# Sixteen stores of converted weight quarters moved out of block 0, and the slots of the preparing work set anew

## The chip, the cores and the metric

The kernel runs on one core of a Trainium2 chip. The metric is the device time of one execution in microseconds (us). The core's engines run their own instruction queues: TensorE (PE) multiplies, VectorE (DVE) and ScalarE (ACT) do elementwise work, GpSimd (POOL) helps with elementwise work between tiles on chip, and SyncE (SP) issues nearly all transfers between DRAM and the chip's memory.

## The reference

```python
# q, k, v: 8 x 8 heads x 576 x 64, attention inside chunks of 64
scores = scale * np.matmul(q_c, k_c.transpose(0, 1, 2, 4, 3))
scores = scores - np.max(scores, axis=-1, keepdims=True)
attn = np.exp(scores)
attn = attn / (np.sum(attn, axis=-1, keepdims=True) + 1e-09)
out = np.matmul(attn, v_c)
...
x = out.transpose(0, 2, 1, 3).reshape(4608, 512)
h = x @ w_in                                  # 512 x 2048
g = h * np.clip(h + 3.0, 0.0, 6.0) / 6.0
return (g @ w_out).astype(np.float32)         # 2048 x 512
```

## The kernel before, in words

The 4608 tokens are nine blocks of 512. Every matrix is held as a rounded part and a remainder, and each product of a 128 x 128 weight tile with 128 x 512 data is three matmuls (`passes`, L361): rounded by rounded, rounded by remainder, remainder by rounded. Blocks 0, 1 and 2 are multiplied plainly. Blocks 3 to 8 go in three pairs; there the two products with w_in and w_out are each computed from seven half-size products (numbers 1 to 7) of sums and differences of weight quarters with sums and differences of data quarters.

The order of work on each engine is the order in which the program issues it. In block 0 that order is a written list, `FIRST` (L52): `W` loads a weight, `H`, `L`, `P`, `A`, `C`, `D` convert it (H, L, C on ACT, P, A, D on DVE), `M` and `N` are the two products, `R`, `G`, `K`, `B` form the gate (R, K on ACT, G, B on DVE), `U` and `X` store converted weights in DRAM, and names that begin with `A1` or `A2` belong to the attention of the next blocks (`A1x` is the last division by the sum). `X5o` is `keep(1, 5)` (L413): it stores quarters of weight 5 of w_out in the DRAM arrays `stream_a` or `stream_b`, from which `fetch` (L470) later brings them, three stretches ahead.

After block 0 the order comes from slots. A slot is six matmuls. `MIDDLE` (L39) has the 32 products of blocks 1 and 2 with w_in at slots -120 to -57, two slots each. The second product of blocks 1 and 2, by the seven products (`second_product`, L801, with s = -1), has slots -56 to -1. The first product of the first pair (`first_product`, L739, with s = 0) starts at slot 0: in each of its eight rounds seven slots, one for each of the products 1, 5, 6, 7, 2, 3, 4. Behind the matmuls of each slot, `tick` (L666) issues what `at` (L620) has put there, in the order of the fractions of the times; what has the same fraction keeps the order in which it was put in, and the tables are put in ahead of what the products themselves add. So a table entry at 4.0 goes before the `relu` of product 7 that is put at slot 4, and one at 4.5 goes behind it.

The tables are these. `MID` has the attention of blocks 2 to 5 (loads, max, subtract, exp, sum, multiply, turn, places, values; the values and the next scores are one visit of PE). `OUT_SUMS` and `IN_SUMS` form the weight sums that the seven products need, for w_out and w_in, one entry for each p (`prepare`, L422). `MID_UNITS` splits the gated data into operands (`units`, L784), `MID_MORE` splits the first pair's x into its seven operands (`x_operands`, L492). Here both give only times; the steps are taken in their fixed order, so the sorted times count. A split is a copy on ACT and a subtraction on DVE; the operand of product 6 has two more subtractions (L507, L508), and the operand of product 7 reads the first of them.

An entry of `IN_SUMS` for p = 3 to 7 has one tile only, `x1`, of which there is a single buffer. Its five times are those of these steps:

```python
nc.sync.dma_start(out=whole[0][0][:, :, 1]..., in_=words[:, p]...)    # L444, SP: load
POOL.tensor_tensor(out=to, in0=x, in1=y, op=op)                       # L453, POOL: four of them
ACT.copy(out=t[:, :, 0], in_=t[:, :, 1].bitcast(F32))                 # L456, ACT
DVE.tensor_tensor(out=t[:, :, 1], in0=..., op=ALU.subtract)           # L459, DVE
nc.sync.dma_start(out=kept(m, p, places), in_=...)                    # L462, SP: store
```

The load of the next p writes the tile that the store of this p reads.

Of the kernel before, what the change touches and what calls it, by code (L numbers as in the profile page):

```python
# [50 lines left out]
PARTED = 2  # L51
FIRST = """  # L52
Q0 S0a S0b I1 T0 m0a m0b Q1 W0i u0a u0b S01 I3 S10 I2 m01 e00 u01 z00 e01 S11 I2 T1 m10 H0i W1i V0 z01 W2i L0i m11 x00 W0o x01 L1i W4 P0i n10 I2 e10 z10 V1 H1i
A0Q W1o A0i n11 e11 z11 t00 t01 I3 W3i c00 v00 c01 x10 L2i L0o W5 v01 I3 h00 C0i h01 x11 t10 t11 I1 P1i c10 A1i C1i D0i c11 M0.00 M0.02 H0o l00 l01 H4 M1.00 v10
v11 M1.01 D1i M1.02 M0.01 P0o H2i P2i A2i h10 h11 M1.10 P4 M1.12 A0o l10 A0T l11 L4 M0.12 C0o W3o M0.10 M0.11 M1.11 C2i A4 A0S L1o R0 D2i C4 G0 M2 D0o H3i P3i
L3i D4 K0 B0 N0 A3i W8 H5 R1 G1 H1o C3i K1 L5 D3i M3 P1o P5 A1o B1 A5 R2 G2 L3o C1o W6 D1o H6 M4 P6 R3 G3 U4 C5 D5 W2o K2 L6 B2 N1 H2o A6 L2o H3o M5 P2o W9 U5
R4 A2o W12 P3o G4 C2o D2o K3 B3 A0m A3o L8 C6 K4 R5 W7 D6 H7 U6 P7 C3o D3o X4i L7 B4 A1Q N2 X4o M6 H8 G5 A7 P8 N3 A8 R6 C7 K5 D7 B5 G6 W10 N4 C8 W13 A0u U7 U8
D8 L9 K6 B6 H10 M7 A0e W11 P10 A0z N5 H9 R7 W14 P9 A9 L10 G7 L11 X6i C9 A0V A0x X8i A0t X1i N6 M8 K7 D9 A10 A0c0 A0c1 U9 M9 A0c2 C10 U10 R8 B7 X9i R9 D10 G8 N7
A0c3 X10i K8 G9 X10o K9 X8o B9 H11 A0c4 B8 H12 P11 M10 X9o R10 A11 C11 P12 G10 N8 A0v X0i L12 W15 A0h U11 A1S X6o D11 K10 N8e X0o M11 A1T N9 L13 A0l A12 C12 U12
D12 X11i L14 R11 B10 X12i N10 H13 A1m P13 X7i M12 G11 A13 A2Q C13 A1u A1e D13 K11 X11o A1z A1x H14 R12 B11 A1V P14 M13 R13 G12 A1t X1o A1c U13 X5i X2o G13 A14  # L60
N11 K12 B12 C14 D14 X3i N11e H15 A1v U14 P15 X3o K13 A1h A1l L15 X14i A15 A2S X13i C15 N12 X2i M14 B13 U15 N13 R14 X5o X7o G14 K14 D15 X15i M15 X14o R15 B14 G15
K15 B15 X15o X12o X13o
""".split()
MID = ((None, -2, -1.0, -1.0, 1.3, 1.6, 2.0, 2.2, (2.35, 2.9, 3.7, 3.75, 3.8), 5.2), (0.5, 4.5, 5.2, 6.15, 6.65, 6.9, 7.9, 9.35, (), 9.5), (5.3, 13.15, 9.8, 10.05, 12.05, 12.8, 12.8, 13.8, (14.5, 14.8, 14.85, 15.15, 15.7), 16.1), (9.9, 16.5, 16.15, 16.5, 17.35, 17.4, 17.8, 17.8, (19.25, 19.3, 20.1, 20.65, 21.2), 21.6), (17.4, 21.05, 21.6, 22.55, 23.15, 23.15, 24.15, 25.05, (25.5, 25.8, 26.1, 26.4, 26.45), 27.2), (25.0, 28.4, 27.45, 27.45, 28.3, 28.5, 28.9, 29.1, (29.55, 29.6, 29.9, 30.45, 31.0), 32.2), (28.5, 32.25, 36.3, 43.8, 43.8, 44.8, 49.0, None, (), None))
OUT_SUMS = ((0, ('A1',), (-124.6, -124.6, -122.6, -115.7, -114.5, -114.0)), (1, ('L1',), (-114.6, -114.6, -110.7, -107.7, -106.7, -106.2)), (2, ('w0_1', 'w1_1'), (-114.5, -112.0, -112.0, -109.6, -109.6, -108.1)), (3, ('w0_1', 'w1_1'), (-105.0, -103.1, -103.1, -100.6, -100.6, -100.1)), (4, ('w2_1', 'w3_1'), (-102.6, -102.6, -102.6, -91.7, -91.7, -91.0)), (6, ('w0_1', 'w1_1'), (-98.7, -91.2, -90.7, -86.5, -86.5, -80.9)), (7, ('w2_1', 'w3_1'), (-88.5, -87.08, -86.44, -84.9, -79.2, -75.7)), (5, ('w0_1', 'w1_1'), (-80.8, -80.8, -80.8, -75.3, -75.3, -75.3)))
ADD_UP = (('A2', (0, 1, 2, 3), (-120.8, -117.8, -117.8, -116.8, -115.1)),)
PARKED = 10
TURNED = ((0, 0), (0, 1), (1, 1), (2, 1))
IN_SUMS = ((0, ('w0_1', 'w1_1'), (-71.5, -67.0, -63.3, -58.3, -56.0)), (1, ('w2_1', 'w3_1'), (-75.0, -72.0, -65.3, -64.8, -57.5)), (2, ('w2_1', 'w3_1'), (-54.5, -54.5, -41.8, -36.8, -35.8)), (3, ('x1',), (-50.0, -50.0, -42.8, -42.8, -38.8)), (4, ('x1',), (-36.5, -33.5, -29.8, -25.3, -25.0)), (5, ('x1',), (-21.0, -11.0, -11.0, -10.5, -10.0)), (6, ('x1',), (-4.0, 4.0, 7.2, 8.2, 10.0)), (7, ('x1',), (15.0, 21.0, 24.2, 25.2, 27.0)))
FETCHES = (19.7, 28.5, 25.5)  # L70
TEMPS = {"p1": "w0_1", "u2": "w1_1", "u4": "w2_1"}
STEADY = ((-0.9, 8.1, 6.1, 0.2, 12.4, 13.9, 17.0, 20.1), (13.1, 20.3, 20.1, 22.0, 23.5, 28.5, 32.2, 41.1), (29.3, 53.1, 41.1, 42.4, 44.5, 46.4, 46.9, 71.8), (65.6, 79.6, 71.8, 75.8, 77.2, 79.4, 79.5, 87.6))
# [2 lines left out]
PLACES = ((12.2, 13.7, 14.7, 15.7, 16.7), (35.2, 36.2, 37.2, 38.2, 39.2), (60.2, 60.7, 62.7, 63.7, 66.7), (82.2, 82.8, 83.4, 83.5, 84.1))  # L75
UNITS = (-3.9, -1.9, -1.8, -1.7, 4.0, 3.9, 5.4, 10.5, 12.5, 12.0, 13.2, 13.5, 16.6, 14.9, 15.4, 17.3, 25.9, 26.1, 27.5, 29.2, 28.5, 32.8, 35.3, 37.1, 39.2, 41.1, 39.3, 43.0)
MORE = (44.4, 45.6, 50.0, 51.5, 51.9, 52.8, 53.8)
MID_UNITS = (-5.5, -5.0, -1.0, -1.5, 12.0, 11.4, 6.4, 4.4, 13.5, 15.0, 18.0, 21.0, 16.1, 18.9, 14.3, 12.7, 34.6, 31.6, 26.5, 27.7, 36.5, 39.2, 33.3, 43.1, 40.7, 43.5, 38.9, 44.2)
MID_MORE = (47.4, 46.2, 49.5, 53.4, 52.8, 56.8, 56.3)


@with_exitstack
def tile_kernel(ctx: ExitStack, tc: tile.TileContext, qk_in, v_in, weights, out):
# [50 lines left out]
    class Convert:  # L134


        def __init__(self, ft, m=None):
            self.ft, self.m = ft, m
            self.n = 512 if ft < HALVED else 1024
# [40 lines left out]
        def store(self):  # L180
            nc.sync.dma_start(out=words[:, self.ft % NFP, 1 - self.ft // NFP].rearrange("p (k t) -> p k t", k=2), in_=self.a[:, :2])
            if self.ft >= PARKED:
                nc.sync.dma_start(out=words_out[:, self.ft % NFP].rearrange("p (k t) -> p k t", k=2), in_=self.a[:, 2:])
# [7 lines left out]
    class Attention:  # L191


        def __init__(self, n, dp, psum=None):
            self.blocks = (n, dp) not in TURNED
            self.n, self.dp = n, dp
# [225 lines left out]
    def prepare(m, p, tags):  # L422
# [9 lines left out]
        if m:  # L432
            parked = p + NFP >= PARKED
            if parked:
# [85 lines left out]
    def visit(a, b):  # L520

        a.multiply(range(2))
        b.scores()
        a.multiplied(range(2))
# [8 lines left out]
    steps = {}  # L533
# [4 lines left out]
    def named(**fs):  # L538
        steps.update(fs)
# [59 lines left out]
    for ft in range(NFT):  # L599
        for m, end in ((0, "i"), (1, "o")) if ft < HALVED else ((None, ""),):  # L600
            c = Convert(ft, m)
            named(**{f"{k}{ft}{end}": f for k, f in zip("WHLPACD", (c.load, c.high, c.low_words, c.shift, c.add, c.cast, c.low))})
            if ft > ADD_UP[-1][1][-1]:
                named(**{f"U{ft}": c.store})
# [15 lines left out]
    def at(slot, *f, rank=0):  # L620

        todo.setdefault(int(slot // 1), []).extend((slot % 1 + rank, g) for g in f)
# [90 lines left out]
    def put_middle():  # L713

        when = lambda t: -SLOTS - 2 * (len(MIDDLE) - t)
        for k, a in enumerate(chain):
            load_qk, load_v, high, sub, exp, total, mult, turn, places, values = MID[k]
            if load_qk is not None:
                at(when(load_qk), a.load_qk)
            at(when(load_v), a.load_v)  # L720
            at(when(high), a.tiles)
            for i, t in enumerate((high, sub, exp, total, mult)):
                at(when(t), lambda i=i, a=a: a.soft(i))
            if turn is None:
                return
            at(when(turn), a.swap if a.blocks else a.transpose)
            for n, t in enumerate(places):
                at(when(t), lambda n=n, a=a: a.place(n))
            a.psum = own_banks
            at(when(values), lambda a=a, b=chain[k + 1]: visit(a, b), finish)  # L730

    def put_sums(m, starts):

        for p, tags, times in starts:
            unit = prepare(m, p, tags)
            for t in times:
                at(t, lambda unit=unit: next(unit))
# [143 lines left out]
    for s in range(-1, NSUP):  # L881
        base = 2 * SLOTS * s
        box = {}

        def unit(k, s=s, box=box):
            if k == 0:
                if s == 0:
                    ring.insert(0, SUM_SLOT)
                box["units"] = units(box["g"], box["t2"])
            next(box["units"])  # L890

        for k, t in enumerate(UNITS if s >= 0 else MID_UNITS):
            at(base + SLOTS + t, lambda k=k, unit=unit: unit(k))
        if s + 1 < NSUP:
            def more(s=s, box=box):
                if "x" not in box:
                    box["x"] = x_operands(s + 1, DVE)
                next(box["x"])

            for t in MORE if s >= 0 else MID_MORE:  # L900
                at(base + SLOTS + t, more)
        if s < 0:
            put_middle()
            for tag, fts, starts in ADD_UP:
                unit = add_up(tag, fts)
                for t in starts:
                    at(t, lambda unit=unit: next(unit))
            put_sums(1, OUT_SUMS)
            put_sums(0, IN_SUMS)
            for t in FETCHES:  # L910
                at(-SLOTS - 2 * (len(MIDDLE) - t), fetch)
            first_products(box)
        else:
            if s + 1 < NSUP:
                put_steady(NSTD + 2 * s + 2, base)
            first_product(s, base, box)
        second_product(s, base + SLOTS)
# [35 lines left out]
```

## Time and profile before

| | |
|---|---|
| median of 3 runs | 778.4 us (777.41 to 778.54) |
| the profiled execution | 779.57 us, of which the span of the instructions is 777.8 us |
| PE busy | 766.6 us, 99% of the span |
| DVE busy | 621.8 us, 80% |
| ACT busy | 409.2 us, 53% |
| POOL busy | 146.8 us, 19% |
| queue of the transfers (q1) | 72.8% of 16 engines' span |

A group line of the profile gives the line of the code, the engine, the operation, the tile written and the tiles read. The timeline gives the start in us from the span's beginning and the duration; in brackets stand the idle time of the engine just before and what ended it. Durations of PE overlap: a matmul lasts 0.39 us and the next starts 0.227 us after it.

### The profile page before, as it was taken

To read this page: it belongs to the slowest core of one execution; us is meant where nothing else is said; L and a number is where in the kernel's file an instruction comes from. 1 tells how busy PE (TensorE), PEld (TensorE's weight loads), DVE (VectorE), ACT (ScalarE), POOL (GpSimd) and SP (SyncE) were. 2 spreads that over 40 slices of the span, in tenths; PEclk is the share of its full clock that TensorE was granted. 3 is DMA by queue.
4 is the path that set the end of the run, shared out by engine and by line. 5 is a ranking of instruction groups with operands and counts; after the bars stand their busy time and mean duration, and the time that the engine had idled before them with its cause. 6 is when DMAs were issued, how large, how long until landed. Compare 5 with 4: busy or idle time off the path is not lost.

```text
span 777.8 us, 13523 instructions
## 1 busy us (share of the span) xinstructions
PE 766.6 (99%) x5489; PEld 627.8 (81%) x5489; DVE 621.8 (80%) x750; ACT 409.2 (53%) x549; POOL 146.8 (19%) x134
## 2 busy tenths in 40 slices
PE   8999999999999999999999999999999999999998
PEld 4788788888788888888888888888888888888886
DVE  6999868799799879787899886777998756669961
ACT  5989646466656534535575534454737323346330
POOL 0000004366453121332200002221100012221000
PEclk9999999999999999999999999999999999999999
DMA  9999987756977889876676777675756766565573
GB/s 362 374 371 346 360 323 277 272 200 245 315 267 237 335 290 309 322 257 212 242 275 208 253 231 244 227 243 187 261 190 207 240 217 195 193 207 204 191 239 112
DMA packets 51837, 199.05 MB, mean 256 GB/s; under 512 B 4672, under 2 KB 10816, under 8 KB 38720
## 3 DMA queue, kind: packets, MB, share of 16 engines
q1 hardware_dynamic: 51488, 197.94, 72.8%
q8 instruction: 43, 0.70, 0.3%
q10 hardware_dynamic: 288, 0.26, 0.1%
q14 instruction: 18, 0.15, 0.0%
HBM read 153.62 MB, written 44.56 MB: 255 GB/s over the span
## 4 chain that ended last, share of the span: by engine, by line
PE 75%; DVE 9%; DMA 7%; ACT 5%; issue 3%; POOL 2%; SPq 0%; ACTq 0%; DVEq 0%; POOLq 0%
PE acc L363 18%; PE acc L364 18%; PE acc L365 18%; PE h L363 6%; PE h L365 6%; PE h L364 6%; PE h L329 2%; DMA a<-hl 2%; DMA hl<-words 2%; POOL hl L453 2%; PE two L234 1%; DVE xop L481 1%; DVE hl L459 1%; DMA x<-qk_in 1%; DVE g L664 1%
## 5 line engine op out<-in xcount | busy, mean ns | idle before, releaser
L363 PE MATMUL acc<-xop,ws 128*128 128x512 f32 x608 | 237.5, 391 | 0.0
L364 PE MATMUL acc<-xop,ws 128*128 128x512 f32 x608 | 236.6, 389 | 0.0
L365 PE MATMUL acc<-xop,ws 128*128 128x512 f32 x608 | 236.6, 389 | 0.0
L363 PEld LDWEIGHTS acc<-xop,ws 128*128 128x128 f32 x608 | 114.1, 188 | 24.3 <-DVE h L630 0.3
L365 PEld LDWEIGHTS acc<-xop,ws 128*128 128x128 f32 x608 | 114.1, 188 | 23.9
L364 PEld LDWEIGHTS acc<-xop,ws 128*128 128x128 f32 x608 | 114.1, 188 | 23.5
L481 DVE TENSOR_TENSOR xop<-g,xop 128x1024 fp32r<-128x1024 f32 x96 | 117.1, 1251 | 7.7 <-ACT xop L480 7.7
L480 ACT CAST xop<-g 128x1024 fp32r<-128x1024 f32 x96 | 96.8, 1052 | 32.1 <-PE acc L365 24.4
L663 ACT ACTIVATE r<-acc,half 128x512 f32<-128x512 f32 x100 | 66.9, 687 | 68.9 <-DVE acc L630 55.8
L664 DVE SCALAR_TENSOR_TENSOR g<-r,acc 128x512 f32<-128x512 f32 x100 | 66.8, 681 | 44.4 <-ACT r L663 41.1
L453 POOL TENSOR_TENSOR hl<-hl 128x256 f32<-128x256 f32 x64 | 56.9, 891 | 213.4 <-DVE hl L439 127.0
L749 POOL TENSOR_TENSOR g<-g 128x512 f32<-128x512 f32 x24 | 31.0, 1293 | 324.8 <-DVE g L664 324.8
L363 PE MATMUL h<-xop,ws 128*128 128x512 f32 x176 | 68.8, 391 | 0.0
L365 PE MATMUL h<-xop,ws 128*128 128x512 f32 x176 | 68.5, 389 | 0.0
L364 PE MATMUL h<-xop,ws 128*128 128x512 f32 x176 | 68.5, 389 | 0.0
L663 ACT ACTIVATE r<-h,half 128x512 f32<-128x512 f32 x28 | 19.3, 690 | 84.2 <-DVE h L630 83.4
L630 DVE TENSOR_TENSOR u<-h,p 128x512 f32<-128x512 f32 x32 | 22.0, 687 | 31.4 <-PE h L365 24.9
L364 PE MATMUL acc<-x,w 128*128 128x512 f32 x112 | 43.8, 391 | 0.8 <-issue 0.8
L363 PE MATMUL acc<-x,w 128*128 128x512 f32 x112 | 44.3, 395 | 0.0
L365 PE MATMUL acc<-x,w 128*128 128x512 f32 x112 | 43.6, 390 | 0.0
L262 ACT ACTIVATE e<-e 128x1024 f32<-128x1024 f32 (+1 forms) x18 | 18.2, 1013 | 48.1 <-DVE e L260 48.1
L363 PEld LDWEIGHTS h<-xop,ws 128*128 128x128 f32 x176 | 33.0, 188 | 7.2 <-ACT xop L480 0.4
(114 smaller groups left out, 1215.9 us busy)
## 6 DMA issues: line engine op xcount, KB each, us to landing
ws<-b SPq DMA_DIRECT2D x56, 1024.0 KB, 4.9
ws<-a SPq DMA_DIRECT2D x24, 1024.0 KB, 5.2
ws<-a SPq DMA_DIRECT2D x24, 768.0 KB, 4.5
qk<-qk_in SPq DMA_DIRECT2D x16, 1024.0 KB, 7.5
w<-w_in_out SPq DMA_DIRECT2D x12, 1024.0 KB, 9.9
v<-v_in SPq DMA_DIRECT2D x17, 512.0 KB, 5.7
out_t<-o SPq DMA_DIRECT2D x30, 256.0 KB, 5.6
b<-hl SPq DMA_DIRECT2D x12, 512.0 KB, 5.0
```

What stands on the lines that cost most here:

```text
L262: ACT.activation(out=flat(self.e), in_=src if self.by_product else flat(self.e), func=AF.Exp, scale=SCALE)
L329: PE.matmul(self.po[s][o, a, i, :], lhsT=self.v[rows, a, i, o], rhs=self.aT[rows, a, i, HALF.index(o)] if self.blocks else self.aT[rows, a ...
L363: PE.matmul(ps, lhsT=a_h, rhs=b_h, start=first, stop=False, skip_group_check=more)
L364: PE.matmul(ps, lhsT=a_h, rhs=b_l, start=False, stop=False, skip_group_check=more)
L365: PE.matmul(ps, lhsT=a_l, rhs=b_h, start=False, stop=last, skip_group_check=more)
L453: POOL.tensor_tensor(out=to, in0=x, in1=y, op=op)
L480: ACT.copy(out=t[:, :, 0], in_=src)
L481: DVE.tensor_tensor(out=t[:, :, 1], in0=src, in1=t[:, :, 0].bitcast(F32), op=ALU.subtract)
L630: return lambda: DVE.tensor_tensor(out=out, in0=x, in1=y, op=ALU.add)
L663: return (lambda: ACT.activation(out=r, in_=ps, func=AF.Relu, bias=half, scale=1.0 / 6.0), lambda: DVE.scalar_tensor_tensor(out=out, in0=r ...
L664: lambda: DVE.scalar_tensor_tensor(out=out, in0=r, scalar=1.0, in1=ps, op0=ALU.min, op1=ALU.mult))
L749: sub = lambda o, x, y: lambda: POOL.tensor_tensor(out=o, in0=x, in1=y, op=ALU.subtract)
```

## The change

It takes sixteen `X` stores (5.5 MB) out of `FIRST` and issues them at slots -120 to -89 instead, by a new table `STORES`. It reorders some steps of `FIRST` and gives new times to `MID`, `OUT_SUMS`, `ADD_UP`, `IN_SUMS`, `MID_UNITS` and `MID_MORE`. No operation is added or taken away. The long lines of `FIRST`, `MID` and `IN_SUMS` are cut here, at the three dots, to the places that are spoken of.

```diff
 FIRST = """
...
-... H3i P3i L3i D4 K0 B0 N0 A3i W8 H5 R1 G1 H1o C3i K1 L5 D3i M3 P1o P5 A1o B1 A5 R2 G2 L3o C1o W6 D1o H6 ...
+... H3i P3i L3i D4 K0 B0 N0 A3i A0T W8 H5 R1 G1 H1o C3i K1 D3i M3 P1o P5 A1o L5 B1 R2 G2 L3o C1o U4 W6 D1o H6 M4 A5 ...
...
-MID = (...
-       (5.3, 13.15, 9.8, 10.05, 12.05, 12.8, 12.8, 13.8, (14.5, 14.8, 14.85, 15.15, 15.7), 16.1),
+MID = (...
+       (5.8, 10.4, 9.55, 9.55, 10.3, 10.3, 12.3, 13.55, (14.25, 14.3, 14.6, 14.65, 15.45), 16.1),
...
+STORES = (('X4i', -120), ('X6i', -118), ('X7o', -117.7), ('X11i', -112), ('X8i', -110), ('X12i', -109.0), ('X14i', -105.0), ('X10i', -104), ('X4o', -102.2), ('X15o', -101.4), ('X15i', -100), ('X5o', -98.5), ('X11o', -95.5), ('X13i', -92.1), ('X1i', -89.0), ('X2i', -89))
...
-IN_SUMS = (... (3, ('x1',), (-50.0, -50.0, -42.8, -42.8, -38.8)), (4, ('x1',), (-36.5, -33.5, -29.8, -25.3, -25.0)), (5, ('x1',), (-21.0, -11.0, -11.0, -10.5, -10.0)), (6, ('x1',), (-4.0, 4.0, 7.2, 8.2, 10.0)), (7, ('x1',), (15.0, 21.0, 24.2, 25.2, 27.0)))
+IN_SUMS = (... (3, ('x1',), (-54.0, -54.0, -42.8, -42.8, -39.8)), (4, ('x1',), (-36.5, -27.5, -27.5, -27.5, -27.5)), (5, ('x1',), (-21.0, -10.0, -10.0, -10.0, 2.0)), (6, ('x1',), (4.0, 4.0, 4.0, 7.2, 7.2)), (7, ('x1',), (15.0, 21.0, 24.2, 25.2, 27.0)))
...
-MID_MORE = (47.4, 46.2, 49.5, 53.4, 52.8, 56.8, 56.3)
+MID_MORE = (56.4, 45.7, 60.5, 60.9, 58.3, 59.8, 50.3)
...
             put_middle()
+            for name, t in STORES:
+                at(t, steps[name])
             for tag, fts, starts in ADD_UP:
```

The times of `MID_MORE` count from slot -56. Sorted, the first pair's seven operands, which PE needs at slots 0 to 6, were split at slots -9.8, -8.6, -6.5, -3.2, -2.6, 0.3 and 0.8, and are now split at -10.3, -5.7, 0.4, 2.3, 3.8, 4.5 and 4.9. The row of `MID` shown is that of block 3, first half. In `MID_UNITS`, one split of the operands of product 6 now goes ahead of the subtraction (L459) of `IN_SUMS` p = 3, and the splits for product 2 stand behind the steps of p = 4.

## Rows read from the trace of the kernel before

**Rows 1.** The page's part 1: busy time, share, instructions.
```profile
PE 766.6 (99%) x5489; PEld 627.8 (81%) x5489; DVE 621.8 (80%) x750; ACT 409.2 (53%) x549; POOL 146.8 (19%) x134
```
**Rows 2.** Waits of PE: us in total, times, longest.
```profile
PE h L329 <- ACT e L294: 0.9, 2, 0.5
...
PE h L363 <- DVE r L554: 0.6, 2, 0.4
PE two L308 <- DVE e L271: 0.4, 1, 0.4
...
PE h L365 <- DVE w L186: 0.2, 1, 0.2
```
**Rows 3.** Timeline of DVE in block 0, ahead of the second such wait.
```profile
35.50 1.22 DVE L170 CUSTOM_DVE_ANT_0 u<-u,r 128x2048 uint16<-128x2048 uint16 x1
36.64 0.68 DVE L554 SCALAR_TENSOR_TENSOR r<-r,h 128x512 f32<-128x512 f32 x1
```
**Rows 4.** Stretches: PE, PEld, DVE, ACT, POOL busy; PE clock; DMA share; GB/s.
```profile
40.00:60.00 20.00, 20.00 (x90) 16.57 (x89) 19.50 (x27) 17.71 (x24) 0.00 (x0) 1.00 1.00 371
...
120.00:140.00 20.00, 20.00 (x208) 16.59 (x207) 16.74 (x24) 13.32 (x21) 5.86 (x8) 1.00 0.76 265
140.00:160.00 20.00, 20.00 (x212) 16.64 (x211) 15.46 (x20) 9.67 (x14) 8.06 (x10) 1.00 0.72 252
```
**Rows 5.** Timeline of PE around slots 0 and 5.
```profile
297.00 0.39 PE L365 MATMUL h<-xop,ws 128*128 128x512 f32 x1
...
297.91 0.39 PE L363 MATMUL acc<-xop,ws 128*128 128x512 f32 x1
...
304.92 0.43 PE L363 MATMUL acc<-xop,ws 128*128 128x512 f32 x1
```
**Rows 6.** Timeline of ACT, the copy of p = 5 and what follows it.
```profile
285.76 1.05 ACT L456 CAST hl<-hl 128x1024 fp32r<-128x1024 f32 x1 [5.64 <-POOL hl L453]
286.72 1.04 ACT L480 CAST xop<-x 128x1024 fp32r<-128x1024 f32 x1
```
**Rows 7.** Timeline of DVE around slot 0.
```profile
295.23 2.48 DVE L496 TENSOR_TENSOR x<-x 128x1024 f32<-128x1024 f32 x2
297.64 2.36 DVE L481 TENSOR_TENSOR xop<-x,xop 128x1024 fp32r<-128x1024 f32 x2
299.92 0.69 DVE L813 TENSOR_TENSOR o<-h,u 128x512 f32<-128x512 f32 x1
```
**Rows 8.** Timeline of SP: stores and loads of the sums.
```profile
244.43 0.32 SPq L462 DMA_DIRECT2D a<-hl  x1
...
252.44 0.37 SPq L444 DMA_DIRECT2D hl<-words  x1
...
267.87 0.32 SPq L462 DMA_DIRECT2D a<-hl  x1
...
272.80 0.38 SPq L444 DMA_DIRECT2D hl<-words  x1
...
313.75 0.42 SPq L462 DMA_DIRECT2D a<-hl  x1
...
321.41 0.37 SPq L444 DMA_DIRECT2D hl<-words  x1
```
**Rows 9.** Line L444, the five loads: time from issue to landing.
```profile
DMA to landing us min/median/max: 5.8/6.8/8.1
```
**Rows 10.** Timeline of POOL, the sums of p = 4 and 5.
```profile
258.45 3.19 POOL L453 TENSOR_TENSOR hl<-hl 128x256 f32<-128x256 f32 x4 [18.55 <-DMA hl<-words]
279.79 5.94 POOL L453 TENSOR_TENSOR hl<-hl 128x256 f32<-128x256 f32 x4 [18.15 <-DMA hl<-words]
```
**Rows 11.** Timeline of PE in the first 18 us.
```profile
1.25 3.54 PE L123 MATMUL h<-r 128*128 128x512 bf16 x8 [1.25 <-DVE half L110]
9.66 0.69 PE L239 MATMUL two<-x 64*64 64x64 f32 x32 [1.59 <-DMA x<-qk_in]
16.93 0.82 PE L123 MATMUL h<-ident 128*128 128x512 bf16 x3
```
## What is predicted, and how it follows

> **What bounds the kernel now.** I read the busy times first: PE is busy 766.6 of 777.8 us [rows 1], so only work that PE does, or time in which it stands, can move the end. Next, PE's own list of waits. Away from the first 10 us it stands only a few times: at two visits of the attention, waiting for the last placement on ACT; at two products of block 0, for a gate on DVE; at one transpose, for the division of the attention; at one weight, for its conversion [rows 2]. That is 0.9 + 0.6 + 0.4 + 0.2 = 2.1 us of idle. Each such wait also breaks the overlap of two matmuls (one lasts 0.39 us, the next starts after 0.227 us), so six of them cost 6 x 0.16 = 1.0 us more: 3.1 us in all is what a better order can win. Third, since nothing else can be won, I looked for what the new order can lose: for every table entry, what stands behind it in its engine's queue, and how soon PE wants that. For this the timelines of ACT, DVE, SP and POOL around slot 0 count. Slot 0 starts at 297.91 and slot 5 at 304.92 [rows 5]; between them PE runs without a gap worth naming.
>
> **The change, part by part.**
>
> *Block 0.* The sixteen stores leave a stretch in which the transfers run at a full share (371 GB/s at 40 to 60 us [rows 4]); 5.5 MB at that rate are 15 us of transfer time. PE hardly waits for transfers there, so the gain is bounded by rows 2. In `FIRST`, A5 (1.2 us on DVE) now stands behind the gate G2 instead of ahead of it; in the trace that gate starts right behind A5, at 36.64 [rows 3], and PE waits for it. That wait should go. The steps of weight 4 that start its conversion, H4 and P4, go one place earlier or more; the weight and the division that PE waits for at the end of block 0 have a freer transfer queue. In `MID` the exp and the sum of block 3's first half are issued about two products earlier (10.3 for 12.05 and 12.8), its multiply half a product and its turn and last placement a quarter: the two visits should lose most of their waits. Of the 3.1 us I take 2.6 as won; the bounds are 1.0 (the gate and its overlap alone, and a part of the visits) and 3.1.
>
> *The stores in their new place.* They fall between slots -120 and -89; counted back from slot 0 at 1.36 us a slot (six times 0.227), with the visits and the rest of block 0's products between, that is roughly 112 to 165 us. SP issues such a store in 0.3 to 0.4 us [rows 8] and has room. The transfers there run at a share of 0.72 to 0.76 [rows 4]: over 53 us that leaves some 14 us, and the stores want 15. So the queue is about full for a while and loads of the attention land later, but each is issued seven slots or more (10 us) ahead of its use. I take 0.4 us lost, with bounds 0 and 2. Were the cover gone, a late load would hold a visit, and with it PE.
>
> *Sums for p = 4.* Load at slot -36.5 as before, but the four sums, the copy, the subtraction and the store all at -27.5. The copy on ACT holds ACT until POOL is done; behind it stands the split for product 2 that PE wants at slot -22. In the trace the sums of p = 4 end at 258.45 + 3.19 = 261.6 [rows 10], some 6 us before slot -22. The subtraction of p = 3 ahead of it moves behind one more split (2.3 us on DVE), and the store and load between them follow. That leaves about 1 us of slack after the copy and two subtractions. I take 0, bounds 0 and 3 us.
>
> *Sums for p = 5 and 6, and the operands of the first pair.* This decides. Before, the load of p = 6 stood at -4, its copy on ACT at 7.2, eleven slots (15 us) later. Now load, sums and copy stand all at 4.0, and the store of p = 5, which has to land before that load may write the same tile, moves from -10 to 2.0. At slot 4 the copy of p = 6 is issued on ACT ahead of the relu of product 7 and ahead of the splits at 4.5 and 4.9, whose operands PE wants at slots 5 and 6. ACT takes its queue in order: the trace shows it at p = 5, where ACT sat idle 5.64 us before its copy, for POOL, and began the split behind it 0.96 us after the copy had begun [rows 6]. There PE wanted that operand 11 us later, so it cost nothing. Now the cover is one slot. Step by step:
>
> 1. DVE. The outgoing sum of product 3 (slot 0) can start when PE has ended the first half, at 297.00 + 0.39 [rows 5], say 297.5, for DVE is no longer in arrears (before it came to it only at 299.92 [rows 7]). Then come, in this order, the subtraction for product 6's operand (1.15 us), two subtractions of x (2.4) and the second outgoing sum (0.6) [rows 7]: 297.5 + 0.6 + 1.15 + 2.4 + 0.6 = 302.25.
> 2. Meanwhile PE. The subtractions for the operands of products 7 and 2 now come behind that on DVE, at 302.25 + 1.15 = 303.4, and, behind two sums of 0.6, at 305.8. PE wants them at about 302.2 and 303.8: it loses 1.2 us at slot 3 and 0.8 at slot 4.
> 3. SP sends the second sum, then the store of p = 5: issued at about 302.9.
> 4. The store lands. From store to the next load in the trace: 8.0, 4.9 and 7.7 us [rows 8]. PE will stand, and the fetches wait for PE, so the queue is emptier than in those rows: I take the middle between the least and the median, 6.3. The load takes 5.8 to 8.1, median 6.8 [rows 9]: by the same choice 6.3. So 302.9 + 12.6 = 315.5.
> 5. Four sums on POOL: 3.2 us at p = 4, 5.9 at p = 5 [rows 10]; I take 3.2, since DVE stands too: 318.7.
> 6. ACT: copy 0.95, relu 0.6, copy of the operand of product 3, 0.95. DVE: its subtraction 1.15. 318.7 + 3.65 = 322.35. The second matmul of slot 5 reads it, 0.23 after the slot's start.
>
> So slot 5 starts in effect at 322.1 where it started at 304.92: 17.2 us later, step 2 included. From below: 302.9 + 4.9 + 5.8 + 3.2 + 3.65 - 0.23 - 304.92 = 15.3. From above, with 8.0, 8.1 and 5.9: 23.6. PE is never idle after that, so nothing gives it back.
>
> *The clock of TensorE.* PE then stands some 15 us. In the trace it stood nowhere so long except before its first matmul. There eight matmuls took 3.54 us, one each 0.42 us; later three took 0.82, one each 0.22 [rows 11]: the lower level, 1.2 GHz, and then the full 2.4. Behind a gap of 1.59 us the next ones were at full speed [rows 11]. A gap of 15 us is nearer to the start than to that, so I take the price of the start: 8 x 0.2 = 1.6 us; bounds 0 and 1.6. The Trainium skill (TensorE: Matmul & The Clock Gate, section The HAM clock gate) says that the slow clock is the default, comes back with idleness and is released by activity; by that the sum is the one below, without it 1.6 us less. No row here shows a gap of that length.
>
> **Sum.** Against the profiled execution: 779.57 - 2.6 + 0.4 + 17.2 + 1.6 = 796.2. That execution lies 1.2 above the median, so the median should be 795.0. With all low bounds: 779.57 - 3.1 + 15.3 - 1.2 = 790.6. With all high ones: 779.57 - 1.0 + 2 + 3 + 23.6 + 1.6 - 1.2 = 807.6.
>
> **The rivals.** What a measurement can tell from no change is 0.2%, 1.6 us: 776.8 to 780.0 is the same.
>
> *All hidden, faster.* ACT is not held at slot 4: the splits for products 3 and 4 run ahead of the copy of p = 6, and DVE keeps up. For this the order at one slot would have to differ from the one that I read (4.0 ahead of 4.5). It decides from the point where each split's subtraction ends before the second matmul of its slot. Then only the gain remains: 779.57 - 2.6 - 1.2 = 775.8. Against it: rows 6.
>
> *DVE alone, the same.* ACT isn't held, but the late splits queue on DVE: step 2's 2.0 us, and 1.3 us more for product 3's operand. 775.8 + 3.3 = 779.1.
>
> *Transfers choke as well, still slower.* The stores fill the queue in blocks 1 and 2, and a load for a visit comes 5 us late, and p = 4 costs its 3: 795.0 + 8 = 803. For it: the 15 us of stores against 14 us of room. Against it: the loads' lead.
>
> **Chances.** Forecast (ACT held at slot 4, 789 to 802 by itself) 0.83; hidden 0.08; DVE alone 0.05; choked as well 0.04. So slower 0.87, same 0.05, faster 0.08. The range 788 to 803 leaves out the two cheap rivals and some tails, about 2 in 10.
>
> **What would show it.** Right: ACT idle for over 10 us just before an L456 copy near 303 to 319 us, with POOL named; POOL waiting for the load, the load for the store; PE idle 10 us or more at a matmul that reads an operand; perhaps slow matmuls behind it. Before that, PE's waits of rows 2 gone and slot 0 some 2 us earlier. Wrong: an L663 or L480 on ACT between the load of p = 6 and its copy, or PE without a gap at slot 5. If the gap is there and another size, it is the two transfers of step 4 that I mis-sized.

## The result and the profile after

The changed kernel takes 790.53 us (median of 6 runs, 789.72 to 791.22), the kernel before 778.47 (6 runs beside it, 777.34 to 781.04): 1.015 times as long, interval 1.013 to 1.017. The execution whose profile follows took 789.72 us, its span 787.7; that of the kernel before is the one of [rows 1].

First the page of the kernel after: part 1, and of part 2 (the span in 40 slices) the busy share of PE and the granted clock.

```profile
PE 768.5 (98%) x5489; PEld 629.0 (80%) x5489; DVE 620.0 (79%) x750; ACT 409.3 (52%) x549; POOL 146.9 (19%) x134
PE   9999999999999993999999999999999999999998
PEclk9999999999999997999999999999999999999999
```

The work is that of [rows 1]. One slice of 19.7 us, from 295 to 315 us, is two thirds empty, and the granted clock is 0.7 in it. Next, PE's waits of the kernel after (us in total, times, longest).

```profile
PE acc L363 <- ACT xop L480: 10.8, 1, 10.8
PE acc L364 <- DVE xop L481: 2.3, 3, 1.1
PE h L363 <- DVE r L554: 0.3, 1, 0.3
```

Of the waits of [rows 2], one of the two for a gate is left; the others are gone. One of 10.8 us has come, for the copy (L480) of an operand, and three of 2.3 us together, for subtractions (L481). Their places, by the timeline of PE:

```profile
292.74 0.39 PE L363 MATMUL acc<-xop,ws 128*128 128x512 f32 x1
...
298.27 0.50 PE L364 MATMUL acc<-xop,ws 128*128 128x512 f32 x1 [1.06 <-DVE xop L481]
...
300.73 0.50 PE L364 MATMUL acc<-xop,ws 128*128 128x512 f32 x1 [0.81 <-DVE xop L481]
...
312.93 0.79 PE L363 MATMUL acc<-xop,ws 128*128 128x512 f32 x1 [10.78 <-ACT xop L480]
314.19 0.79 PE L364 MATMUL acc<-xop,ws 128*128 128x512 f32 x1 [0.47 <-DVE xop L481]
314.78 0.63 PE L365 MATMUL acc<-xop,ws 128*128 128x512 f32 x1
315.21 0.63 PE L363 MATMUL acc<-xop,ws 128*128 128x512 f32 x1
...
317.33 0.40 PE L365 MATMUL acc<-xop,ws 128*128 128x512 f32 x1
317.57 0.40 PE L363 MATMUL acc<-xop,ws 128*128 128x512 f32 x1
```

Slot 0 starts at 292.74, the second matmuls of slots 3 and 4 come late by 1.06 and 0.81, and slot 5 waits for a copy on ACT. The matmuls behind the gap start 0.43 us apart, those from 317.33 on 0.24. Who held that copy is read on SP, POOL, ACT and DVE, in the order in which one waited for the other:

```profile
296.40 0.68 DVE L813 TENSOR_TENSOR o<-h,u 128x512 f32<-128x512 f32 x1
297.50 0.42 SPq L462 DMA_DIRECT2D a<-hl  x1
302.33 0.37 SPq L444 DMA_DIRECT2D hl<-words  x1
307.15 3.12 POOL L453 TENSOR_TENSOR hl<-hl 128x256 f32<-128x256 f32 x4 [26.96 <-DMA hl<-words]
310.31 1.04 ACT L456 CAST hl<-hl 128x1024 fp32r<-128x1024 f32 x1 [13.00 <-POOL hl L453]
311.26 0.68 ACT L663 ACTIVATE r<-h,half 128x512 f32<-128x512 f32 x1
311.84 1.98 ACT L480 CAST xop<-x 128x1024 fp32r<-128x1024 f32 x2
312.91 2.36 DVE L481 TENSOR_TENSOR xop<-x,xop 128x1024 fp32r<-128x1024 f32 x2 [11.63 <-ACT xop L480]
```

This is the chain of the prediction's steps 1 to 6: the second outgoing sum on DVE, the store of p = 5, the load of p = 6 when it has landed, four sums on POOL, the copy, the relu, the copy of the operand, its subtraction. ACT stood 13.00 us with the relu and the operand's copy queued behind the copy of p = 6.

Where the 10 us of span come from, by the start of the first matmul of a slot (us, from the two timelines of PE):

| slot | before | after | after - before |
|---|---|---|---|
| -120 | 111.99 | 109.28 | -2.7 |
| -66 | 202.39 | 198.20 | -4.2 |
| -56 | 219.50 | 214.07 | -5.4 |
| 0 | 297.91 | 292.74 | -5.2 |
| 11 | 313.18 | 323.75 | +10.6 |
| 20 | 325.57 | 335.99 | +10.4 |

So 5.2 us are won before slot 0 and 15.7 lost between slots 0 and 11; from there to the end the kernel after wins 0.6 us back.

Not all of the 5.2 us is the change's. Up to slot -11 the run e4 below issues the same steps in the same order as the kernel before, and so is a second execution of it; in the same way e1 to e3, e5 to e7 and e9 to e11 are further ones of the kernel after. The two of the old order reach slot -56 at 219.50 (before) and 217.86 us (e4), the ten of the new at 213.99 to 216.23, nine of them by 214.53. So against e4 the change wins 3.8 us there, and 1.6 us more is the slow profiled execution of before. Nor does the load of x, for which PE stood 1.59 us before [rows 11] and 0.4 after, come earlier by the change; in e4 it is as early:

```profile
8.31 0.69 PE L239 MATMUL two<-x 64*64 64x64 f32 x32 [0.44 <-DMA x<-qk_in]
```

and slot -120 starts there at 111.68, only 0.3 us earlier than before.

### The profile page after: what moved, and what is told of

Read it like the earlier page. It is cut to its first block, busy times and chain, and to the rows that moved or that the text cites. A ratio compares the mean times of both kernels' runs of the same rounds, so it can differ in the third digit from the quotient of the medians.

```text
span 787.7 us, 13514 instructions
## 1 busy us (share of the span) xinstructions
PE 768.5 (98%) x5489; PEld 629.0 (80%) x5489; DVE 620.0 (79%) x750; ACT 409.3 (52%) x549; POOL 146.9 (19%) x134
## 4 chain that ended last, share of the span: by engine, by line
PE 94%; DMA 2%; DVE 1%; ACT 1%; POOL 0%; issue 0%; SPq 0%; POOLq 0%; ACTq 0%
PE acc L363 23%; PE acc L364 22%; PE acc L365 22%; PE h L363 7%; PE h L365 7%; PE h L364 7%; PE h L329 2%; PE two L234 2%; DMA x<-qk_in 1%; DMA a<-hl 1%; DMA hl<-words 1%; PE two L239 0%; POOL hl L453 0%; PE two L308 0%; DVE x L496 0%
## 5 line engine op out<-in xcount | busy, mean ns | idle before, releaser
L363 PE MATMUL acc<-xop,ws 128*128 128x512 f32 x608 | 238.3, 392 | 10.8 <-ACT xop L480 10.8
L481 DVE TENSOR_TENSOR xop<-g,xop 128x1024 fp32r<-128x1024 f32 x96 | 119.2, 1273 | 6.6 <-ACT xop L480 6.6
L480 ACT CAST xop<-g 128x1024 fp32r<-128x1024 f32 x96 | 97.2, 1052 | 35.5 <-PE acc L365 25.7
L363 PEld LDWEIGHTS h<-xop,ws 128*128 128x128 f32 x176 | 33.0, 188 | 6.9
L365 PEld LDWEIGHTS h<-xop,ws 128*128 128x128 f32 x176 | 33.0, 188 | 6.9
```

Of the source, the lines that this page charges most:

```text
L363: PE.matmul(ps, lhsT=a_h, rhs=b_h, start=first, stop=False, skip_group_check=more)
L365: PE.matmul(ps, lhsT=a_l, rhs=b_h, start=False, stop=last, skip_group_check=more)
L480: ACT.copy(out=t[:, :, 0], in_=src)
L481: DVE.tensor_tensor(out=t[:, :, 1], in0=src, in1=t[:, :, 0].bitcast(F32), op=ALU.subtract)
```

## The experiments

Each is the kernel before or after with one table row or a few set otherwise, unless it says more. Ratios are to the kernel before, run on the same chip, with their intervals.

**Which of the two late things holds PE.** The first four put back the rows of the sums, the times of the operands, both, or put the new sums alone into the kernel before.

*e1_sums_back*, in the kernel after:

```diff
-(5, ('x1',), (-21.0, -10.0, -10.0, -10.0, 2.0)), (6, ('x1',), (4.0, 4.0, 4.0, 7.2, 7.2))
+(5, ('x1',), (-21.0, -11.0, -11.0, -10.5, -10.0)), (6, ('x1',), (-4.0, 4.0, 7.2, 8.2, 10.0))
```

> The changed kernel, with only the rows of IN_SUMS for p = 5 and 6 as before (store of p = 5 at -10, load of p = 6 at -4, its copy on ACT at 7.2). Theory (ACT held by the copy of p = 6): the idle of 10.8 us at slot 5 is gone and with it the slow clock; the late operands stay and cost some 3.5 us at slots 3 to 5 on DVE: about 778 to 779 us. Rival (the late operands alone make the delay): little changes, 788 us or more.

Measured: 782.32 us (9 runs), ratio 1.0049 (1.003 to 1.0068). The wait of 10.8 us is gone, as expected, but the time stays 3 to 4 us above the kernel before, not at it (by the medians 3.2, by the ratio 3.8). PE in the first pair's first round, and the clock over two stretches there (the columns are those of [rows 4]):

```profile
299.46 0.51 PE L363 MATMUL acc<-xop,ws 128*128 128x512 f32 x1 [0.84 <-ACT xop L480]
301.32 0.50 PE L364 MATMUL acc<-xop,ws 128*128 128x512 f32 x1 [1.36 <-DVE xop L481]
...
303.81 0.80 PE L364 MATMUL acc<-xop,ws 128*128 128x512 f32 x1 [0.64 <-DVE xop L481]
304.40 0.63 PE L365 MATMUL acc<-xop,ws 128*128 128x512 f32 x1
...
307.33 0.80 PE L364 MATMUL acc<-xop,ws 128*128 128x512 f32 x1 [0.46 <-DVE xop L481]
...
312.19 0.63 PE L363 MATMUL acc<-xop,ws 128*128 128x512 f32 x1
312.62 0.50 PE L364 MATMUL acc<-xop,ws 128*128 128x512 f32 x1
```
```profile
299.30:302.58 3.28, 1.77 (x6) 1.23 (x7) 3.25 (x6) 1.05 (x2) 3.12 (x3) 1.00 0.55 214
302.58:306.00 3.42, 2.78 (x7) 1.50 (x5) 1.79 (x3) 1.60 (x3) 1.69 (x2) 0.50 0.65 211
```

The late operands alone make PE stand 0.84 + 1.36 + 0.64 + 0.46 = 3.3 us, which is the price that the rival "DVE alone" gave them. But behind the first two of these waits the granted clock also goes from 1.00 to 0.50, its lower level of 1.2 GHz, and 18 matmuls from 303.81 to 312.19 start at that pace; at 0.2 us each that is some 3.6 us, a term that the rival's sum left out. Slots 0 to 11 take 24.0 us in this run, 8.7 more than before; PE also waits 0.9 us for weights ahead of slot 0.

*e2_operands_back*, in the kernel after:

```diff
-MID_MORE = (56.4, 45.7, 60.5, 60.9, 58.3, 59.8, 50.3)
+MID_MORE = (47.4, 46.2, 49.5, 53.4, 52.8, 56.8, 56.3)
```

> The changed kernel, with only MID_MORE as before: all seven operands are split ahead of the copy of p = 6. Theory (ACT held): ACT is held as long as before, but PE now runs on until it needs a bank whose gate stands behind the copy, at slot 8 (round two, product 5), so some 10 us of idle appear there in place of slot 5: about 785 to 788 us. Rival (the late operands alone): about 774 us, no idle over 1 us.

Measured: 788.52 us (4 runs), ratio 1.0118 (1.0102 to 1.0133), slightly above the expected stretch. With the operands early again PE runs on through slot 7; in front of slot 8 it stands nearly as long as ever, for a gate. PE's wait in this run:

```profile
PE acc L363 <- DVE g L664: 10.1, 1, 10.1
```

The relu that this gate needs is the one behind the copy of p = 6, ahead of which ACT stands 15.38 us for POOL in this run. So the held ACT is enough by itself; the late operands set at which slot PE meets it and cost some 2 us (788.52 against 790.53).

*e3_both_back* has both edits, in the kernel after: the tables `IN_SUMS` p = 5, 6 and `MID_MORE` are those of before, everything else is new.

> The changed kernel with both of these as before: IN_SUMS p = 5 and 6, and MID_MORE. What is left of the change is the 5.2 us by which slot 0 came earlier in its trace. Theory: 778.5 - 5.2 = 773.3 us, no idle of PE over 1 us after 15 us. Rival (the moved stores choke the transfers behind slot 0): still over 778 us.

Measured: 778.50 us (10 runs), ratio 0.9999 (0.9983 to 1.0014), a miss by 5 us, at the rival's number: the 10 to 12 us are gone, but in the time nothing of the 5 us won before slot 0 is left. ACT, DVE and PE in this run:

```profile
281.70 1.05 ACT L456 CAST hl<-hl 128x1024 fp32r<-128x1024 f32 x1 [8.27 <-POOL hl L453]
283.73 1.23 DVE L481 TENSOR_TENSOR xop<-g,xop 128x1024 fp32r<-128x1024 f32 x1 [3.48 <-ACT xop L480]
```
```profile
PE h L363 <- DVE o L813: 1.7, 1, 1.7
```

Here it is the copy of p = 5, at -11 and so ahead of the last unit and the first operand in the new order, that holds ACT for 8.27 us (in [rows 6] 5.64). DVE stands 3.48 us for the unit queued behind it, comes to slot 0 in arrears, and PE waits for its outgoing sum. Slot 0 itself starts at 295.04, 2.3 us later than in the kernel after, with a wait of 0.9 us for weights just ahead. That this one row costs all that the earliness won isn't shown: e2, where the copy stands at -10, has the same wait of 1.7 us for the outgoing sum.

*e4_sums_alone*, in the kernel before: only the rows of p = 5 and 6 are the new ones.

> The kernel before with only the rows of IN_SUMS for p = 5 and 6 as in the change. Theory (ACT held by the copy of p = 6, alone enough): PE runs to slot 8 and stands there for some 12 us, then has about 1.6 us of slow clock: 789 to 793 us. Rival (it needs the late operands or the moved stores too): 778 to 780 us.

Measured: 790.80 us (4 runs), ratio 1.0151 (1.0125 to 1.0176), as expected. PE's wait:

```profile
PE acc L363 <- DVE g L664: 9.8, 1, 9.8
```

The two rows alone, in a kernel whose stores and operands are as before, make the time as long as the whole change does. Between slots 0 and 11 they lose 12.4 us; the kernel after, with late operands and in the new order, loses 15.7.

**The transfers, the row of p = 6 and the clock.**

*e6_two_transfers*, in the kernel after: the store of p = 5 is issued at -10 and the load of p = 6 at -4, so that both transfers are over before slot 4; sums and copy stay at 4.0.

```diff
-(5, ('x1',), (-21.0, -10.0, -10.0, -10.0, 2.0)), (6, ('x1',), (4.0, 4.0, 4.0, 7.2, 7.2))
+(5, ('x1',), (-21.0, -10.0, -10.0, -10.0, -10.0)), (6, ('x1',), (-4.0, 4.0, 4.0, 7.2, 7.2))
```

> The changed kernel with only two transfers issued earlier: the store of p = 5 at -10 and the load of p = 6 at -4, as before the change; the sums and the copy of p = 6 stay at 4.0. Theory (ACT is held for as long as load and sums are late): the load can go some 11 us earlier, so the copy begins near 305 instead of 310 us, slot 5 about 6 to 7 us earlier, the slow clock is shorter or gone: 782 to 785 us. Rival (the place of the copy alone, not the transfers): 790 us.

Measured: 785.68 us (4 runs), ratio 1.0099 (1.0079 to 1.0118); the profiled execution, 788.62, is the longest of them. SP, POOL and ACT in it:

```profile
293.27 0.38 SPq L444 DMA_DIRECT2D hl<-words  x1
...
302.45 5.68 POOL L453 TENSOR_TENSOR hl<-hl 128x256 f32<-128x256 f32 x4 [18.45 <-DMA hl<-words]
308.15 1.05 ACT L456 CAST hl<-hl 128x1024 fp32r<-128x1024 f32 x1 [4.03 <-POOL hl L453]
```

ACT stands 4.03 us instead of 13.00. Counted from slot 0 (297.77 here) the copy of p = 6 starts after 10.4 us, not 17.6: 7.2 us of the hold were the two transfers; the rest is that ACT's own work ahead of it ended later. The time falls by 5 us only. The load took 9.2 us to POOL, the four sums 5.68, and PE stood 2.2 us for weights ahead of slot 0: by their order on SP the store and load now share the queue with the fetches for it. The sums took 3.12 in the kernel after, while DVE did nothing; here DVE was at work:

```profile
302.00:308.50 6.50, 3.44 (x13) 2.02 (x12) 6.07 (x8) 2.34 (x3) 5.44 (x4) 1.00 0.38 117
```
```profile
307.00:310.30 3.30, 0.00 (x0) 0.00 (x0) 0.00 (x0) 0.00 (x0) 2.89 (x4) 0.50 0.00 0
```

The first stretch is of this run (DVE busy 6.07 of 6.50), the second of the kernel after (DVE 0.00). The Trainium skill (SBUF — State Buffer, section SBUF: two separate sides) states that GpSimd and a DVE operation with two operands in that memory take turns at shared ports, one standing still meanwhile; 5.68 against 3.12 us for the same four sums agrees.

*e10_p6_row*, in the kernel after: the store of p = 5 at -10 and the whole row of p = 6 as before, operands late as in the kernel after.

```diff
-(5, ('x1',), (-21.0, -10.0, -10.0, -10.0, 2.0)), (6, ('x1',), (4.0, 4.0, 4.0, 7.2, 7.2))
+(5, ('x1',), (-21.0, -10.0, -10.0, -10.0, -10.0)), (6, ('x1',), (-4.0, 4.0, 7.2, 8.2, 10.0))
```

> The changed kernel with the store of p = 5 at -10 and the whole row of p = 6 as before (load -4, sums 4, copy 7.2, subtraction 8.2, store 10); the first three steps of p = 5 stay where the change put them, behind the last unit and the first operand. What is left of the loss is the late operands: 1.2, 1.0 and some 1.3 us at slots 3, 4 and 5. Theory: 790.5 - 15.9 + 3.5 = 778 us, and slot 0 at 293 us. Rival (the early slot 0 is taken back by something else, as in the run with both rows back): 781 us or more.

Measured: 782.30 us (4 runs), ratio 1.0055 (1.0039 to 1.0072): the rival's side. ACT isn't held at p = 6 any more, nor at p = 5 ahead of the last unit; what remains are the late operands (waits of 0.84, 1.37, 0.48 and 0.76 us in slots 3 to 5) and slow matmuls between 303.45 and 306.44. Slots 0 to 11 take 21.4 us, 6.1 more than before. Something else takes back a part too: slot 0 starts at 294.76 and not at 293, with a wait of 0.7 us for weights ahead of it. The time is e1's, without e1's copy at -11, so in e1 too most of the cost was not that copy.

*e9_p6_and_operands* is e10 with the operands' times of before:

```diff
-MID_MORE = (56.4, 45.7, 60.5, 60.9, 58.3, 59.8, 50.3)
+MID_MORE = (47.4, 46.2, 49.5, 53.4, 52.8, 56.8, 56.3)
```

> As the run with the row of p = 6 back and the store of p = 5 at -10, and MID_MORE as before too. Theory: what held the run with both rows back was the copy of p = 5 at -11, ahead of the last unit and the first operand; here it stands at -10, behind the last unit, so DVE comes to slot 0 without arrears and the 5 us won before slot 0 are kept: about 774 us, faster than both kernels. Rival (DVE can't split seven operands there in time wherever p = 5 stands): 777 to 779 us.

Measured: 777.09 us (12 runs, 775.01 to 779.23), ratio 0.9982 (0.9971 to 0.9993). The profiled execution took 775.17 us, with slot 0 at 292.71 and slot 8 at 304.52 (before 309.1), and no wait of PE behind slot 0 over 0.6 us:

```profile
PE h L363 <- DVE o L813: 0.6, 1, 0.6
```

The profiled execution ends 4.6 us before that of the kernel before, but it is one of the fastest of its kernel; over the runs 1.3 us of median are won. The median is thus the rival's (777 to 779) and not the 774 expected: e9 keeps a part of what was won before slot 0. It has the lowest median of this study, and its interval lies below the kernel before.

*e7_kept_busy*, the kernel after with 48 matmuls more between slots 4 and 5, whose result nothing reads, to keep TensorE at work while the operand is late:

```diff
+                if (s, p, k) == (0, 0, 5):
+                    warm_up(48)
```

> The changed kernel with 48 matmuls on constants (as those of the warm-up) put between slots 4 and 5, about 10.4 us of work in the 10.8 us in which PE stood; their result is not used. Theory (the idle costs the clock as well as its own length): the matmuls behind it run at 0.227 instead of 0.43 us, the granted clock stays at 1.0, and the time falls by 1.6 us to 789 us. Rival (slow matmuls there have another cause, such as late operands): no change, 790.5 us, and the granted clock as before.

Measured: 788.80 us (4 runs), ratio 1.0138 (1.0125 to 1.0151), 1.7 us below the kernel after, as expected. PE's timeline, and a stretch of this run and the same one of the kernel after:

```profile
302.30 10.53 PE L123 MATMUL h<-ident 128*128 128x512 bf16 x48
313.41 0.50 PE L363 MATMUL acc<-xop,ws 128*128 128x512 f32 x1 [0.58 <-ACT xop L480]
...
315.24 0.40 PE L363 MATMUL acc<-xop,ws 128*128 128x512 f32 x1
315.48 0.39 PE L364 MATMUL acc<-xop,ws 128*128 128x512 f32 x1
```
```profile
292.70:324.00 31.30, 28.12 (x123) 18.08 (x122) 18.34 (x22) 8.49 (x11) 6.39 (x6) 1.00 0.55 190
```
```profile
292.70:324.00 31.30, 18.19 (x69) 13.53 (x69) 17.09 (x22) 8.62 (x11) 6.39 (x6) 0.78 0.52 178
```

With PE kept at work the granted clock stays at 1.00 and the matmuls behind the wait start 0.23 to 0.24 us apart; without, 0.78 and eight of them at 0.43. Slot 5 starts as late as ever: 20.4 us behind slot 0, in the kernel after 20.2. This measures the clock's part by itself: slots 5 to 11 take 9.34 us, in the kernel after 10.82, 1.5 us less. The 1.7 us between the medians agree with it, though the intervals of the two ratios overlap.

**The store alone, the stores of block 0 alone, later sums.**

*e5_store_back*, in the kernel after: only the store of p = 5 goes back to -10.

```diff
-(5, ('x1',), (-21.0, -10.0, -10.0, -10.0, 2.0))
+(5, ('x1',), (-21.0, -10.0, -10.0, -10.0, -10.0))
```

> The changed kernel with only the store of p = 5 at -10 instead of 2.0. Theory (the chain store, load, sums, copy sets the length of the hold): the load of p = 6, still at 4.0, no longer waits for the store's landing, only for the fetch of slot 3 ahead of it on SP, and goes some 2 us earlier; the idle at slot 5 shrinks from 10.8 to about 8.6 us: 788 to 789 us. Rival (the store was not on the chain): 790.5 us.

Measured: 792.71 us (4 runs), ratio 1.0173 (1.015 to 1.0197): a miss, for nothing is won; the median is 2.2 us above the kernel after, though the intervals of the two ratios overlap. SP in this run, and two of PE's waits:

```profile
284.73 0.33 SPq L462 DMA_DIRECT2D a<-hl  x1
...
303.08 0.33 SPq L475 DMA_DIRECT2D ws<-a  x1
303.45 0.43 SPq L444 DMA_DIRECT2D hl<-words  x1
```
```profile
PE acc L363 <- ACT xop L480: 9.1, 2, 8.3
...
PE acc L363 <- DMA ws<-a: 1.3, 1, 1.3
```

The store is 13 us earlier, and the load is issued 1.1 us later than in the kernel after (302.33). It is queued on SP behind the fetch that waits for PE to have done with slot 3; and PE comes there later, because it first stands 1.3 us for weights and the outgoing sums are late too: DVE waits 6.08 us until an earlier outgoing store has landed and starts the sum only at 295.51 (292.26 in the kernel after). So the store isn't alone in holding the load: with it out of the way, the place of the load behind slot 3 does. The theory that the early store shortens the stall was wrong.

*e8_stores_alone*, in the kernel before: the sixteen stores leave `FIRST` and are issued by `STORES`, all else as before.

> The kernel before with only the sixteen stores taken out of FIRST and put at the slots of STORES. Theory (the stores themselves matter little; what was won before slot 0 came from the order of the steps): between 777 and 779 us, no change that can be told. Rival (the freer transfers in block 0 are the gain): 775 us or less. Second rival (the stores choke blocks 1 and 2): over 780 us.

Measured: 780.87 us (12 runs, 777.89 to 782.69), ratio 1.0019 (1.0004 to 1.0034). PE's waits in it:

```profile
PE h L330 <- ACT e L295: 1.8, 2, 1.6
...
PE acc L365 <- DVE x L352: 0.8, 1, 0.8
```

(Lines stand one further here.) Slot -120 comes at 110.04 us, 2.0 earlier than before, slot -56 at 221.09, 1.6 later: in between the visit at slot -88 waits 1.57 us for a placement on ACT and then runs on at the lower clock, so that it takes 6.51 us for 4.24 (columns of [rows 4]; the clock is the 0.50):

```profile
170.30:172.30 2.00, 2.00 (x75) 1.88 (x69) 0.39 (x1) 1.83 (x4) 1.91 (x3) 0.50 1.05 375
```

Against e4, with slot -56 at 217.86, it is 3.2 us later there. The median lies over 780, which is the second rival's side, though the whole difference is 0.2%. The transfers are indeed fuller, a share of 0.95 from 140 to 150 us (before, from 142 to 152, 0.65); that the late placement comes from it isn't tested. Block 0 gains by the stores' leaving, and blocks 1 and 2 lose as much or more; in the change, which also sets the attention's steps anew, they don't.

*e11_later_sums*, in the kernel after: operands as before, and sums that leave the steps of p = 6 and 7 room.

```diff
-(6, ('x1',), (4.0, 4.0, 4.0, 7.2, 7.2)), (7, ('x1',), (15.0, 21.0, 24.2, 25.2, 27.0))
+(6, ('x1',), (4.0, 10.0, 12.2, 13.2, 15.0)), (7, ('x1',), (21.0, 26.0, 29.2, 30.2, 32.0))
-MID_MORE = (56.4, 45.7, 60.5, 60.9, 58.3, 59.8, 50.3)
+MID_MORE = (47.4, 46.2, 49.5, 53.4, 52.8, 56.8, 56.3)
```

> The changed kernel with MID_MORE as before, the store of p = 5 left late (2.0), and the sums behind it moved later instead of earlier: p = 6 at 4.0, 10.0, 12.2, 13.2, 15.0 and p = 7 at 21.0, 26.0, 29.2, 30.2, 32.0. Theory: the copy of p = 6 has eight slots (11 us) behind its load and holds nobody, and the large store and load don't meet the fetches of slot 0, which made the other repaired kernel vary: about 774 us, faster than the kernel before. Rival (a lead of eight slots is too short, or the operands' splits alone bound it): 778 us or more.

Measured: 777.75 us (12 runs, 776.76 to 779.51), ratio 0.9988 (0.9975 to 1.0001). The store at 2.0 and the load at 4.0 stay where the change put them; with the copy eight slots behind the load ACT isn't held (it goes at 312.71, right behind a relu), and against e2, which has the same operands, 10 to 11 us are gone. So it is the lead of the copy over its load that counts, not the place of the load. Of the 4 to 5 us expected to be won against the kernel before, 0.9 came, and the interval includes none: the rival's side, with 778. In this run PE waits 0.6 us for the outgoing sum behind slot 0 and at one visit, at 356 us, 0.8 us for a gate on DVE.

## Why the prediction was right

**The mechanism** was the one forecast: the copy of p = 6, issued at the slot of its own load, holds ACT and what is queued behind it. e2, e4 and e11 show it from three sides: the new rows alone cost 1.0151 times; with the operands early the same stall stands three slots further on (in front of slot 8); and with the copy eight slots behind the load it is gone, the load's place unchanged (e11 against e2).

**Step by step.** Slot 0 came 5.17 us earlier than before, so the prediction's times are read less 5.17. Step 1, the second outgoing sum ends: 302.25 - 5.17 = 297.08; measured 296.40 + 0.68 = 297.08. Step 2, the late operands: 1.2 and 0.8 of idle; measured 1.06 and 0.81. Step 3, the store issued: 297.7; measured 297.50. Step 4, its landing and that of the load: 12.6 us; measured 307.15 - 297.50 = 9.65. Step 5: 3.2; measured 3.12, with DVE standing, which was the ground for choosing the lower of [rows 10]. Step 6, from POOL's end to the second matmul of slot 5: 3.65; measured 314.19 - 310.27 = 3.92.

**What was mis-sized.** Two terms, by 3 us each and both toward a longer time, and each beyond the bound that it was given. First, step 4, the term of 6.3 + 6.3: the store took 4.83 us to the load's issue and the load 4.82 to POOL, where [rows 8] and [rows 9] had 4.9 and 5.8 at the least. The ground given, an emptier queue, holds for the load only:

```profile
297.50:302.33 4.83, 3.08 (x11) 1.91 (x11) 3.75 (x5) 0.00 (x0) 0.00 (x0) 1.00 0.99 357
302.33:307.15 4.82, 0.00 (x0) 0.00 (x0) 0.00 (x0) 0.00 (x0) 0.00 (x0) 0.64 0.69 241
```

While the store ran, the share of the transfers was 0.99 (0.96 and 0.99 in the rows of before that took 8.0 and 4.9 us); while the load ran, it was 0.69 (0.97 there). So the store's 4.83 us doesn't follow from the reason given. The chain costs 14.2 us for 17.2, below its lower bound of 15.3: from slot 0 to the second matmul of slot 5 it is 21.45 for 24.44. (The upper bound was added up wrongly as well: 8.0, 8.1 and 5.9 give 23.4, not 23.6.) Second, the gain before slot 0: 2.6 less 0.4 was taken, and 5.2 was seen. Against e4 it is 3.8 up to slot -56 (2.4 of it in block 0), still above the bound of 3.1 that the waits of [rows 2] gave. The prediction's list of them left out three: 0.2 and 0.2 us for DVE, and 0.85 us at 208 us that the trace puts down to no engine. That last one isn't the old order's own: e4 has none, and e6, with the new order, has one of 0.96 at 205 us. Which of the reordered steps won the rest isn't shown. With both as this pair of executions has them: 796.2 - 3.0 - 3.0 = 790.2, against 789.72 measured. Median against median the forecast is 4.5 us too high (795.0 for 790.53). The measured median lies at the prediction's sum of all low bounds, 790.6; the forecast held because its range began 2.6 us lower, at 788.

**The clock.** 1.6 us taken; seen were eight matmuls at 0.43 us, and 1.5 us less from slot 5 to 11 in e7. The choice of the price of the start over that of [rows 11]'s short gap held. The rule weighed there of the Trainium skill (TensorE: Matmul & The Clock Gate, section The HAM clock gate), that idleness brings the slow clock back and activity releases it, agrees with both traces.

**The stores' new place** was priced at 0.4 lost in sum with 2.6 won. e8 shows that the cost depends on the rest: alone they lose 3.5 us between slots -120 and -56 (4.9 against e4); with `MID` and the sums set anew nothing there is lost. p = 4 cost nothing, as taken: no wait of PE near slot -22 in the kernel after.

**The rivals.** "All hidden" falls by the 13.00 us of ACT. "DVE alone" had its idle right (3.3 us, e1) but left out the clock, and such kernels end at 782.3 and not 779.1 (e1, e10), a wait of 0.7 to 0.9 us for weights included. "Transfers choke as well" did not come: the visits at slots -88 and -77 take 3.48 us each in the kernel after, 4.24 and 4.27 before, 3.48 and 4.14 in e4.

**Still open.** Runs of one kernel spread over 3 to 5 us whatever the change (before 777.0 to 781.65 in 23 runs on one chip, e3 777.6 to 780.84, e9 775.01 to 779.23); why, isn't settled, so a gain of 4.6 us between two executions can be 1.3 in the median. What ends the idle stretch near 205 us, where there is one, is open. Why the slow stretch lasted 9 us in e1 and 3 us in e10, behind nearly the same waits, and why none came in e6 behind the same two, is open too.

## What to carry to other kernels

In a queue that is taken in order, a copy that waits for another engine's result of a fresh load must be issued as many slots behind that load as the load and that engine take together (here 4.82 + 3.12 us, six slots, at a transfer share of 0.69 during the load, and more if the load itself waits for a store); what it costs otherwise is read from the instructions queued behind it. Moving one wait away shows only where the stall is met next: check where the same hold falls on another product, and what stands ahead of the moved transfer on its own queue. Late operands cost their idle time and, in e1 and e10, slow matmuls behind them, so a short wait isn't always priced by its own length alone. And a gain read from two single executions has to be held against a second execution of the same order before it is put down to the change.

## What the runs showed of the hardware

Behind two waits of 0.84 and 1.36 us, one matmul apart, the granted clock was 0.50 in e1 (from 302.58 us on), although neither was as long as the 1.59 us that left it at full in [rows 11]; in e6 the same two waits and a third of 0.86 left it at 1.00, and it fell behind the fourth, of 1.76; in e3 a single one of 1.75 us left it at 1.00, and in e8 a single one of 1.57 us, within a visit, was followed by 0.50 (170.30 to 172.30). In the kernel after a store of 1 MB took 4.83 us at a transfer share of 0.99 and a load of half of that 4.82 us at 0.69. Where the store was issued ahead of slot 0, PE waited there 0.7 to 2.2 us for weights in e1, e3, e5, e6 and e10, but not in e8, e9 and the kernel before. Four sums on POOL took 3.12 us while DVE stood and 5.68 while it worked.
